# Reordering the last steps of a decode kernel: bias row and its sums ahead of the last PV drain, turned V blocks in pieces of 14 and 10

## The chip, the cores and the metric

The kernel runs on one core of one Trainium2 chip. Kernels are compared only within the same rounds. The metric is the device time of one execution in microseconds (us); several runs are timed and their median is quoted. The profiled execution of the kernel before has a span of 1264.1 us, beside a time of 1265.85 us for that run; times within a trace are counted from the start of its span.

A word on the clock: the profile gives the "granted clock" of TensorE, in parts of its full speed.

## The reference, cut to what matters

One token attends to a cache of 65,536 positions, with 16 query heads on 8 key/value heads of size 256; a small token MLP runs beside it; a gate mixes the two.

```python
q = (x @ wq).reshape(B, Sq, 16, 256).transpose(0, 2, 1, 3)
scores = einsum("bhqd,bhkd->bhqk", q, k) * 256 ** -0.5     # k, v: 8 heads, repeated twice
o = einsum("bhqk,bhkd->bhqd", softmax(scores), v)
a = o.transpose(0, 2, 1, 3).reshape(B, Sq, 4096) @ wo       # -> 448 numbers
b = token_mlp(x)                                            # layernorm, w1, gelu, w2, biases
return g * a + (1 - g) * b                                  # g = sigmoid(sum(x * gate_w))
```

K and V together are about 537 MB in bf16, and each byte is used once.

## The kernel before: the parts that the change touches

The kernel streams K and V through SBUF, 48 chunks of each, and keeps the DMA queue filled. The change concerns only the last V chunk, 80 blocks of 128 keys for the last head pair, and the steps after it. That chunk is loaded in four pieces, and the last two slices of `wo` come behind it:

```python
TURN = 24
TAIL = 4
# ...
edges = [0, nlast - TURN - SB, nlast - TURN, nlast - TAIL, nlast]   # 0, 40, 56, 76, 80
for k in range(len(edges) - 1):
    lo, hi = edges[k] * DH, edges[k + 1] * DH
    sp.dma_start(out=vlast[:, lo:hi], in_=src[:, lo:hi]).then_inc(s_last[k], 16)
# ... then wo for r = 0 and r = 1, 224 KB each, on s_wl[0] and s_wl[1]
```

The first 56 blocks go through TensorE "upright" (P as weights, V streamed, summed in `pv`). VectorE drains `pv` into `og`, and `o_turn` turns that into a column. The last 24 blocks go through "turned": the V block is the weight and P is two columns wide, so that the result lands as a column without any drain. `heads` then scales by the softmax denominators and the gate and writes `oT`, the weights of the 16 last matmuls against `wo`.

```python
upright(edges[0], edges[1])
# ... denominators: den_ps, then rden on VectorE
pe.wait_ge(s_last[1], 16)
upright(edges[1], edges[2]).then_inc(s_fp, 1)
dve.wait_ge(s_fp, 2)
drain_pv(False).then_inc(s_fd, 1)                 # og <- pv + og
dve.tensor_scalar(out=row[:], in0=acc[0:1, 0:D], scalar1=bias[:, 0:1], ...).then_inc(s_fd, 1)
pe.wait_ge(s_fd, 1)
o_turn(2)
pe.wait_ge(s_last[2], 16)
turned(edges[2], edges[3])                        # 20 blocks, 2 matmuls each
pe.wait_ge(s_last[3], 16)
turned(edges[3], edges[4]).then_inc(s_fp, 1)      # 4 blocks
dve.wait_ge(s_fp, 3)
heads().then_inc(s_fd, 1)                         # oT <- o_ps * rden
pe.wait_ge(s_fd, 2)
for a in range(4):                                # the sums of the bias row
    pe.matmul(acc4[32 * a:32 * a + 1, 0:DQ], lhsT=one_f[:, 0:1], rhs=row[:, DQ * a:DQ * (a + 1)],
              start=True, stop=False, tile_position=(0, 32 * a), ...)
pe.wait_ge(s_fd, 3)
for k in range(4):                                # r, cc = divmod(k, 2): 16 matmuls with wo
    # at cc == 0: pe.wait_ge(s_wl[r], 16)
    ...
dve.tensor_copy(out=res[0:97, :], in_=acc4[0:97, 0:DQ])   # the cast; then the store
```

The row (everything but the last head pair: earlier heads, MLP, bias) lies in one partition. The four sums spread it over four partitions of `acc4`, where the `wo` matmuls add to it.

The softmax here doesn't subtract the row's maximum and nothing guards it: scores larger than these inputs give would overflow.

## Time and profile before

| | us |
|---|---|
| time, median of the first 3 runs (range) | 1265.99 (1265.82 to 1266.15) |
| span of the profiled execution | 1264.1 |
| TensorE busy / VectorE busy | 722.2 / 675.3 |
| work after the third V piece has landed, to the cast's end | about 2.8 |

The following lines are from the first two parts of the page. The last two are one figure for each of 40 equal slices: the mean busy share of the 16 DMA engines in tenths, and GB/s.

```profile
span 1264.1 us, 10623 instructions
PE 722.2 (57%) x4296; PEld 276.3 (22%) x4296; DVE 675.3 (53%) x462; ACT 50.1 (4%) x127; POOL 78.5 (6%) x111
DMA  9999999999999999999999999999999999999998
GB/s 407 425 435 429 442 435 424 439 433 432 440 430 426 436 434 437 440 426 434 438 427 438 430 436 436 430 432 436 430 443 429 429 439 434 429 442 430 430 436 348
```

The kernel is a stream of bytes with compute hidden under it. In the stretch that the change touches, only what happens after the last bytes can cost time of its own. This is the end of the chain of waits (start, duration, what). In the lines, PE is TensorE, PEld its weight loads, DVE VectorE, and L751 line 751 of that kernel's file:

```profile
1228.07 30.50 DMA kbuf<-in_A_v_cache_dram
1258.57 0.05 issue
1258.62 1.44 PE misc L751 x48
1260.06 0.48 PE acc L789 x8
1260.54 0.50 PE acc L799 x16
1261.06 0.27 DVE res L806
```

The chain goes from a V piece to the 48 turned matmuls, then the eight TensorE passes of the four bias sums, the `wo` matmuls and the cast. The same stretch in the timeline (start, duration, engine, line, operation, count, idle time before it and what ended that):

```profile
1255.40 0.23 DVE L558 TENSOR_SCALAR rden<-rden,gate 128x2 f32<-128x2 f32 x1
1256.22 0.69 DVE L543 TENSOR_TENSOR og<-pv,og 128x512 f32<-128x512 f32 x1 [0.59 <-PE pv L740]
1256.83 0.66 DVE L776 TENSOR_SCALAR row<-acc,bias 1x448 f32<-1x448 f32 x1
1256.97 1.02 PEld L685 LDWEIGHTS misc<-mask,og 128*128 128x128 f32 x8 [1.30 <-DVE og L543]
1258.61 1.36 PEld L751 LDWEIGHTS misc<-pT,kbuf 128*128 128x128 bf16 x48 [0.62 <-DMA kbuf<-in_A_v_cache_dram]
1259.99 0.55 PE L789 MATMUL acc<-row,one_f 1*1 1x112 f32 x8
1260.09 0.16 DVE L550 TENSOR_TENSOR oT<-misc,rden 128x4 bf16<-128x4 f32 x1 [2.60 <-PE misc L751]
1260.46 0.28 PEld L799 LDWEIGHTS acc<-wo,oT 128*1 128x1 bf16 x16 [0.38 <-DVE oT L550]
1261.06 0.27 DVE L806 CAST res<-acc 97x112 bf16<-97x112 f32 x1 [0.81 <-PE acc L799]
```

Two things can be read here. The 48 turned matmuls start when the 20-block piece lands (when its load's semaphore is full), and run past the landing of the 4-block piece. And `heads` ends at 1260.25, but the `wo` matmuls start only at 1260.46, 0.21 us later; after the drain, which ends at 1256.91, TensorE started within 0.06 us. Between `heads` and `wo`, the sums sit on TensorE.

The view of stretches shows the granted clock at that time (stretch and its length; busy us and instructions of TensorE, of its weight loads, of VectorE, ScalarE and GpSimd; the granted clock; the DMA share; GB/s):

```profile
1258.00:1258.50 0.50, 0.07 (x1) 0.00 (x0) 0.00 (x0) 0.00 (x0) 0.00 (x0) 1.00 0.92 350
1258.50:1259.00 0.50, 0.38 (x14) 0.39 (x15) 0.00 (x0) 0.00 (x0) 0.00 (x0) 0.64 0.59 217
1259.00:1259.50 0.50, 0.50 (x25) 0.50 (x23) 0.00 (x0) 0.00 (x0) 0.00 (x0) 0.50 0.17 50
```

The clock falls to half at about 1258.6.

### The profile page before, as it was taken

The page shows a single profiled execution, that of the slowest core. Times are in us where ns is not written, and L with a number is a line of the kernel's source. Part 1 is how long each engine was busy: PE and PEld are TensorE (multiplying, and loading weights), DVE is VectorE, ACT ScalarE, POOL GpSimd, SP SyncE. Part 2 cuts the span into 40 slices and gives each one's busy share as a digit, 9 for nine tenths or more (in the row PEclk, how much of TensorE's full clock was granted, in tenths as well). Part 3 has the DMA queues.
Part 4 walks back from the last instruction along what each step waited for, and adds up shares of the span by engine and source line. Part 5 has one row for each costly group of instructions (what it writes and reads, how often), then busy time and mean ns, then how long its engine had stood idle before and what let it go on. Part 6 is the DMA issues. An engine that isn't in the chain of part 4 may idle for free. (4 is left out here: it accounts for less than half of the span.)

```text
span 1264.1 us, 10623 instructions
## 1 busy us (share of the span) xinstructions
PE 722.2 (57%) x4296; PEld 276.3 (22%) x4296; DVE 675.3 (53%) x462; ACT 50.1 (4%) x127; POOL 78.5 (6%) x111
## 2 busy tenths in 40 slices
PE   3855656456554665556654564555645656466556
PEld 1311222122221222112221221222212222122212
DVE  5745554465544555455555555464545645465544
ACT  0000000000000000000000000000000000000000
POOL 1001010110110101101011011000000000000000
PEclk9887777878787787777878787777877778778887
DMA  9999999999999999999999999999999999999998
GB/s 407 425 435 429 442 435 424 439 433 432 440 430 426 436 434 437 440 426 434 438 427 438 430 436 436 430 432 436 430 443 429 429 439 434 429 442 430 430 436 348
DMA packets 16840, 544.30 MB, mean 431 GB/s; under 512 B 1856, under 2 KB 3906, under 8 KB 4162
## 3 DMA queue, kind: packets, MB, share of 16 engines
q1 hardware_dynamic: 16744, 544.22, 99.7%
q8 instruction: 2, 0.03, 0.0%
q10 hardware_dynamic: 90, 0.01, 0.0%
q14 instruction: 4, 0.03, 0.0%
HBM read 544.22 MB, written 0.00 MB: 431 GB/s over the span
## 5 line engine op out<-in xcount | busy, mean ns | idle before, releaser
L661 PE MATMUL sc<-kT,qw 128*128 128x512 bf16 x2048 | 573.5, 438 | 482.9 <-PEq L657 482.9
L532 DVE STREAM_TRANSPOSE kT<-kbuf 128x2048 f32<-128x2048 f32 x256 | 572.8, 2285 | 330.1 <-DVEq L524 330.1
L661 PEld LDWEIGHTS sc<-kT,qw 128*128 128x128 bf16 x2048 | 211.1, 108 | 845.1 <-issue 692.8
L675 PE MATMUL pv<-vbuf,pT 128*4 128x512 bf16 x2008 | 121.2, 390 | 28.8 <-PEq L705 28.7
L543 DVE TENSOR_TENSOR og<-pv,og 128x512 f32<-128x512 f32 x40 | 27.7, 692 | 98.5 <-DVEq L524 97.9
L608 ACT ACTIVATE p_t<-sc 128x512 bf16<-128x512 f32 x48 | 28.7, 597 | 1191.9 <-PE sc L661 1191.9
L675 PEld LDWEIGHTS pv<-vbuf,pT 128*4 128x4 bf16 x2008 | 47.1, 88 | 99.3 <-issue 53.8
L589 DVE STREAM_TRANSPOSE pT<-p_t 128x512 bf16<-128x512 bf16 x32 | 22.8, 712 | 74.1 <-DVEq L524 74.1
L635 POOL TENSOR_SCALAR t_b<-t_b 128x448 f32<-128x448 f32 x14 | 7.9, 564 | 359.1 <-ACT t_b L617 359.1
L639 POOL TENSOR_SCALAR t_b<-t_b,hw 128x448 f32<-128x448 f32 x14 | 8.9, 638 | 334.0 <-ACT t_b L625 334.0
L579 DVE STREAM_TRANSPOSE pT<-p_t 128x512 bf16<-128x512 bf16 x8 | 5.7, 712 | 26.9 <-DVEq L524 26.9
L720 PE MATMUL acc<-wo,oT 128*1 128x448 bf16 x28 | 10.1, 504 | 12.7 <-PEq L717 12.7
L644 POOL TENSOR_TENSOR ymix<-ymix,t_b 128x448 f32<-128x448 f32 x14 | 16.1, 1148 | 1.1
L638 POOL TENSOR_TENSOR t_b<-t_b,u_b 128x448 f32<-128x448 f32 x14 | 15.8, 1127 | 1.2
L643 POOL TENSOR_TENSOR t_b<-t_b,u_b 128x448 f32<-128x448 f32 x14 | 15.8, 1126 | 1.2
L542 DVE COPY og<-pv 128x512 f32<-128x512 f32 x8 | 5.5, 692 | 18.9 <-DVEq L524 18.9
L594 DVE STREAM_TRANSPOSE pT<-p_t 128x512 bf16<-128x512 bf16 x8 | 5.7, 712 | 14.9 <-DVEq L524 14.9
L617 ACT ACTIVATE t_b<-h_bc,b1T,w1T 128x448 f32<-128x448 f32 x14 | 10.5, 748 | 0.0
L631 POOL TENSOR_SCALAR u_b<-h_bc,w1T,b1T 128x448 f32<-128x448 f32 x14 | 10.0, 715 | 4.1 <-DVE hw L428 2.7
L608 ACT ACTIVATION_READ_ACCUMULATOR p_t<-sc 128x1 f32 x48 | 9.3, 194 | 0.0
L685 PEld LDWEIGHTS misc<-mask,og 128*128 128x128 f32 x64 | 8.7, 196 | 2.4 <-DVE og L543 1.3
L477 DVE TENSOR_TENSOR qw<-qr,block 128x32 bf16<-128x32 f32 (+1 forms) x18 | 8.6, 561 | 0.1
(86 smaller groups left out, 77.4 us busy)
## 6 DMA issues: line engine op xcount, KB each, us to landing
kbuf<-in_A_k_cache_dram SPq DMA_DIRECT2D x32, 5120.0 KB, 33.2
vbuf<-in_A_v_cache_dram SPq DMA_DIRECT2D x31, 5120.0 KB, 20.4
kbuf<-in_A_k_cache_dram SPq DMA_DIRECT2D x16, 6144.0 KB, 35.7
vbuf<-in_A_v_cache_dram SPq DMA_DIRECT2D x16, 6144.0 KB, 23.5
wo<-in_A_wo_dram SPq DMA_DIRECT2D x7, 448.0 KB, 23.6
vbuf<-in_A_wq_dram SPq DMA_DIRECT2D x1, 3072.0 KB, 10.3
kbuf<-in_A_v_cache_dram SPq DMA_DIRECT2D x1, 2560.0 KB, 26.0
kbuf<-in_A_v_cache_dram SPq DMA_DIRECT2D x1, 1280.0 KB, 30.5
```

The source lines that it names most:

```text
L532: dve.transpose(out=kT[b][:].bitcast(FP32), in_=kn[:, s * SB * 128:(s + 1) * SB * 128]).then_inc(s_kt, 1)
L543: return dve.tensor_tensor(out=og[:], in0=pv[:], in1=og[:], op=ALU.add)
L589: dve.transpose(out=pT[:], in_=p_t[:]).then_inc(s_pt, 1)
L608: ins = act.activation(out=p_t[:], in_=sc[:], func=ACT.Exp, scale=scale, accum_out=den[:, c:c + 1])
L617: ins = act.activation(out=t_b[:], in_=h_bc[:], func=ACT.Square, scale=w1T[:, b:b + 1], bias=b1T[:, b:b + 1],)
L631: lambda: pool.tensor_scalar(out=u_b[:], in0=h_bc[:], scalar1=w1T[:, b:b + 1], scalar2=b1T[:, b:b + 1], op0=ALU.mult, op1=ALU.add,),
L638: lambda: pool.tensor_tensor(out=t_b[:], in0=t_b[:], in1=u_b[:], op=ALU.mult),
L643: lambda: pool.tensor_tensor(out=t_b[:], in0=t_b[:], in1=u_b[:], op=ALU.mult),
L644: lambda: pool.tensor_tensor(out=ymix[:], in0=ymix[:], in1=t_b[:], op=ALU.add),
L661: ins = pe.matmul(sc[:], lhsT=qw[:, q, at:at + 128], rhs=kv[:, :, q // 2, :, q % 2], start=(first and q == 0), stop=(last and q == 7), ski ...
L675: ins = pe.matmul(pv[32 * a:32 * a + 4, :], lhsT=pT[:, k, :, ROW0 + s], rhs=vt[:, j * DH:(j + 2) * DH], start=first and k < 4, stop=last a ...
L720: ins = pe.matmul(acc[0:1, 0:D], lhsT=oT[:, k:k + 1], rhs=wo[:, r, cc, :], start=False, stop=False, skip_group_check=True,)
```

## The change

Its intent is to shorten the chain after the last bytes. The row and its four sums move from between `heads` and `wo` to before the last drain, where both engines wait for V. And the 24 turned blocks come in pieces of 14 and 10, so that more of their matmuls run before the last V piece lands. No byte and no instruction is added or taken away, apart from the waits.

```diff
-TAIL = 4
+TAIL = 10
...
         pe.matmul(
             acc[0:1, 0:D], lhsT=col_f[:], rhs=ymix[:], start=False, stop=True, skip_group_check=True,
-        )
+        ).then_inc(s_fp, 1)
+        dve.wait_ge(s_fp, 1)
+        dve.tensor_scalar(
+            out=row[:], in0=acc[0:1, 0:D], scalar1=bias[:, 0:1], scalar2=None, op0=ALU.add
+        ).then_inc(s_fd, 1)
         take(pe, s_pt)
... (upright, denominators, upright; counts of s_fp one higher)
         drain_pv(False).then_inc(s_fd, 1)
-        dve.tensor_scalar(
-            out=row[:], in0=acc[0:1, 0:D], scalar1=bias[:, 0:1], scalar2=None, op0=ALU.add
-        ).then_inc(s_fd, 1)
         pe.wait_ge(s_fd, 1)
+        for a in range(4):
+            pe.matmul(
+                acc4[32 * a:32 * a + 1, 0:DQ], lhsT=one_f[:, 0:1], rhs=row[:, DQ * a:DQ * (a + 1)],
+                start=True, stop=False, tile_position=(0, 32 * a), skip_group_check=True,
+            )
+        pe.wait_ge(s_fd, 2)
         o_turn(2)
... (turned, turned, heads)
-        pe.wait_ge(s_fd, 2)
-        for a in range(4):
-            pe.matmul(
-                acc4[32 * a:32 * a + 1, 0:DQ], lhsT=one_f[:, 0:1], rhs=row[:, DQ * a:DQ * (a + 1)],
-                start=True, stop=False, tile_position=(0, 32 * a), skip_group_check=True,
-            )
         pe.wait_ge(s_fd, 3)
```

More of the change, by code (lines that the diff above doesn't have):

```diff
@@ L769, in critical @@
         ).then_inc(s_fp, 1)
-        dve.wait_ge(s_fp, 1)
+        dve.wait_ge(s_fp, 2)
         rden_gate(den_ps[:, 0:2])
@@ L773, in critical @@
         upright(edges[1], edges[2]).then_inc(s_fp, 1)
-        dve.wait_ge(s_fp, 2)
+        dve.wait_ge(s_fp, 3)
         drain_pv(False).then_inc(s_fd, 1)
-        dve.tensor_scalar(
-            out=row[:], in0=acc[0:1, 0:D], scalar1=bias[:, 0:1], scalar2=None, op0=ALU.add
-        ).then_inc(s_fd, 1)
         pe.wait_ge(s_fd, 1)
+        for a in range(4):
[4 more added lines that the diff above has]
+        pe.wait_ge(s_fd, 2)
         o_turn(2)
@@ L784, in critical @@
         turned(edges[3], edges[4]).then_inc(s_fp, 1)
-        dve.wait_ge(s_fp, 3)
+        dve.wait_ge(s_fp, 4)
         heads().then_inc(s_fd, 1)
-        pe.wait_ge(s_fd, 2)
-        for a in range(4):
-            pe.matmul(
-                acc4[32 * a:32 * a + 1, 0:DQ], lhsT=one_f[:, 0:1], rhs=row[:, DQ * a:DQ * (a + 1)],
-                start=True, stop=False, tile_position=(0, 32 * a), skip_group_check=True,
-            )
         pe.wait_ge(s_fd, 3)
@@ L804, in critical @@
         ins.then_inc(s_fp, 1)
-        dve.wait_ge(s_fp, 4)
+        dve.wait_ge(s_fp, 5)
         dve.tensor_copy(out=res[0:97, :], in_=acc4[0:97, 0:DQ]).then_inc(s_fd, 1)
```

## The prediction

> **What bounds the kernel.** The page's DMA row reads 9 tenths in all but the last of 40 slices, 431 GB/s on average, while TensorE is busy 57% and VectorE 53% of the span. The chain of waits that ended last is 2.4% DMA (30.50 us for the third piece of the last V chunk) and only about 2.5 us of work behind it. The change moves no byte more or less and acts only after about 1250 of 1264.1 us.
>
> **The tail before** (timeline; issue starts plus the times to landing of the DMA view). The four V pieces are issued at 1227.12, 1227.60, 1228.07 and 1228.55. The 20-block piece lands near 1258.57, the 4-block piece near 1259.23, and the two halves of wo (issued 1229.02 and 1229.49, 30.9 and 31.0 us to landing) near 1260.0 and 1260.4. The 48 turned matmuls start at 1258.61 and are issued in 1.36 us, 28 ns each, then the eight bias-row matmuls at 1259.99, heads on VectorE 1260.09 to 1260.25, the 16 wo matmuls from 1260.46 (issued over 0.28 us), the cast at 1261.06, the store at 1261.36.
>
> **What the change does, costed.**
> 1. Pieces of 14 and 10. Between the last two landings 4 blocks took 0.66 us, so 10 blocks take about 1.6 us (estimate): the 14-block piece lands near 1257.6, the last piece still near 1259.2. The turns of og (1256.97 to 1257.99) now end later than that landing, so 28 turned matmuls run from about 1258.0 and end by 1258.8. The last 20 start at 1259.25 and are issued in 0.57 us: done at 1259.82 instead of 1259.97. Gain for heads: 0.15 us.
> 2. Bias row and its sums ahead. The 0.66 us tensor_scalar runs near 1254.7 to 1255.3 in place of 1256.83; rden then follows by 1255.95, still before the drain's start at 1256.22. The eight sums fall between the last upright matmul (1255.8) and the drain's end (1256.91), where TensorE sat idle 0.80 us. Before, the wo matmuls started 0.21 us after heads ended, while the turns of og started 0.06 us after the drain: the sums held TensorE for about 0.15 us. That is removed.
> 3. The new limit. Points 1 and 2 together would start the wo matmuls near 1260.15, but the second half of wo lands only at 1260.4. Its eight matmuls then start near 1260.45, not 1260.60. So of about 0.3 us freed, I expect only 0.15 us to arrive at the end.
>
> **Clock.** The granted clock fell to 0.50 at about 1258.6 (windows view: 0.64 in 1258.5 to 1259.0, 0.50 after). The Trainium skill, "TensorE: Matmul & The Clock Gate", Part 1, says that the clock is halved after an idle window of about 3.4 us whose phase is free-running; so this may fall elsewhere, worth some tenths either way.
>
> **Predicted:** 1265.8 us, from 1265.0 to 1266.6 (8 in 10), mostly run-to-run spread. Chances: faster by over 2% 0.002, within 2% 0.996, slower by over 2% 0.002.
>
> **What would show it:** the turned matmuls split into 28 and 20 with an idle wait on DMA of about 0.4 us between; no bias-row sums between heads and wo; the wo matmuls split into two groups of eight with a DMA wait on wo between.
>
> **What would make it wrong:** the last pieces landing at other times, the sums delaying the drain or the turns of og, a different clock phase, or the wo landing not being the limit (then 0.3 us).

## The result, and the profile after

| | before | after |
|---|---|---|
| median of 6 runs each, us | 1265.99 | 1265.80 |
| range, us | 1265.80 to 1266.15 | 1265.38 to 1266.00 |
| ratio after / before, 95% interval | | 0.9998 (0.9986 to 1.0011) |

Ratios and intervals here and below are worked out from the fast runs of the same rounds; they are not quite the ratio of the medians quoted. The timed difference is not resolved: the interval is more than ten times as wide as the effect, and in a second set of rounds the order was reversed (below). So the argument has to be made inside the traces.

The end of the chain of waits in the changed kernel:

```profile
1229.03 29.98 DMA kbuf<-in_A_v_cache_dram
1259.01 0.04 issue
1259.05 0.69 PE misc L751 x20
1259.74 0.02 issue
1259.77 0.17 DVE oT L550
1259.94 0.04 issue
1259.98 0.60 PE acc L800 x13
1260.58 0.02 issue
1260.61 0.28 DVE res L807
```

Only 20 turned matmuls are left on the chain, and the sums are gone from it. The timeline of the changed kernel:

```profile
1254.92 0.68 DVE L763 TENSOR_SCALAR row<-acc,bias 1x448 f32<-1x448 f32 x1
1255.88 0.23 DVE L558 TENSOR_SCALAR rden<-rden,gate 128x2 f32<-128x2 f32 x1
1255.99 0.37 PE L782 MATMUL acc<-row,one_f 1*1 1x112 f32 x8
1256.26 0.69 DVE L543 TENSOR_TENSOR og<-pv,og 128x512 f32<-128x512 f32 x1
1257.86 0.89 PEld L751 LDWEIGHTS misc<-pT,kbuf 128*128 128x128 bf16 x28
1259.05 0.59 PEld L751 LDWEIGHTS misc<-pT,kbuf 128*128 128x128 bf16 x20 [0.30 <-DMA kbuf<-in_A_v_cache_dram]
1259.77 0.16 DVE L550 TENSOR_TENSOR oT<-misc,rden 128x4 bf16<-128x4 f32 x1 [2.82 <-PE misc L751]
1259.98 0.31 PEld L800 LDWEIGHTS acc<-wo,oT 128*1 128x1 bf16 x16 [0.35 <-DVE oT L550]
1260.61 0.28 DVE L807 CAST res<-acc 97x112 bf16<-97x112 f32 x1 [0.68 <-PE acc L800]
```

The 48 turned matmuls are split into 28 and 20, with a wait for DMA between. The `wo` matmuls start 0.05 us after `heads` ends (1259.93 to 1259.98). The merged line of the 16 `wo` weight loads hides a hole, which shows when the timeline of that engine is asked for from 1260.15 on:

```profile
1260.19 0.10 PEld L800 LDWEIGHTS acc<-wo,oT 128*1 128x1 bf16 x8
```

The second eight wait for the second half of `wo`. In these traces the semaphore of each of these loads is incremented 16 times, and full with the last; in this trace the last increment for the last half of `wo` comes at 1260.15, and the matmuls that need it start at 1260.19.

**What can be compared between traces.** The last landing itself moves from run to run: 1260.41 in the trace of before, 1260.15 in that of after. That is not the change's doing (see the repeats below). So all traces are compared by what follows the last landing: from it to the start of the cast 0.65 us before and 0.46 us after; from it to the end of the span 3.65 us and 3.45 us. The tail became 0.2 us shorter, 0.016% of the time. The two traces are not at the same clock, though: before fell to half at 1258.64, after at 1259.85. What that is worth is asked below.

### The profile page after: what moved, and what is told of

It reads as the page before. It is cut to its first block, busy times and chain, and to the rows that moved or that the text cites. A ratio compares the mean times of both kernels' runs of the same rounds, so it can differ in the third digit from the quotient of the medians.

```text
span 1263.6 us, 10623 instructions
## 1 busy us (share of the span) xinstructions
PE 718.4 (57%) x4296; PEld 275.5 (22%) x4296; DVE 675.1 (53%) x462; ACT 50.1 (4%) x127; POOL 78.5 (6%) x111
## 5 line engine op out<-in xcount | busy, mean ns | idle before, releaser
L452 PE MATMUL sc<-vbuf,xw 128*128 128x512 bf16 x32 | 9.2, 456 | 0.0
## 6 DMA issues: line engine op xcount, KB each, us to landing
kbuf<-in_A_v_cache_dram SPq DMA_DIRECT2D x1, 1024.0 KB, 27.2
```

The costliest lines, as they stand in the source:

```text
L452: last = e.matmul(q_ps[:], lhsT=xw[:, k, HKV - 1 - n:HKV - 1 - n + 128], rhs=rhs, start=(n == 0 and k == 0), stop=(n == HKV - 1 and k >= K ...
```

## The experiments

Twelve experiments were run. With before and after they make 14 traces of ten different kernels. The table collects their tails. "Last V" is the last increment of the last V piece, "last landing" the last increment of any load; both are read from the trace's semaphore records, as is the time from which the clock is at half. The other columns are worked out from the starts and ends in the timeline, rounded as they are printed, so they can be off by 0.01 us.

| kernel | last landing, us | half clock from | `heads` start after last V | first `wo` matmul after `heads` end | cast after last landing | end of span after last landing |
|---|---|---|---|---|---|---|
| before | 1260.41 | 1258.64 | 0.89 | 0.21 | 0.65 | 3.65 |
| before_again | 1260.36 | 1259.98 | 0.88 | 0.21 | 0.69 | 3.68 |
| after | 1260.15 | 1259.85 | 0.76 | 0.05 | 0.46 | 3.45 |
| after_again | 1260.38 | 1260.52 | 0.76 | 0.05 | 0.41 | 3.40 |
| order_only | 1260.30 | 1257.49 | 0.90 | 0.05 | 0.54 | 3.53 |
| order_only_b | 1260.35 | 1259.07 | 0.91 | 0.05 | 0.51 | 3.50 |
| pieces_only | 1260.54 | 1260.19 | 0.76 | 0.12 | 0.47 | 3.47 |
| pieces_only_b | 1260.53 | 1260.54 | 0.75 | 0.05 | 0.45 | 3.45 |
| sums_twice | 1260.51 | 1260.45 | 0.87 | 0.31 | 0.77 | 3.78 |
| tail16 | 1260.46 | 1260.13 | 1.08 | 0.05 | 0.75 | 3.74 |
| tail20 | 1260.24 | 1257.94 | 1.32 | 0.05 | 0.93 | 3.93 |
| wo_first | 1260.30 | 1258.74 | 0.77 | 0.06 | 1.59 | 4.59 |
| wo_three | 1260.47 | 1259.56 | 0.78 | 0.05 | 0.43 | 3.42 |
| before_warm | 1260.58 | 1262.03 | 0.87 | 0.06 | 0.36 | 3.36 |

The two theories at the outset: (T) the sums held TensorE, the last turned matmuls held `heads`, and once both are shorter the last half of `wo` is the limit; (R) one of the two parts, or mere semaphore latency, accounts for it all. All runs computed the right result.

### The parts alone, a repeat, and the sums doubled

**order_only**: the changed kernel with the old sizes.

```diff
-TAIL = 10
+TAIL = 4
```

> The new order with pieces of 20 and 4. Theory (the sums held TensorE between heads and the wo matmuls, and the last wo landing is the new limit): the gap from the end of heads to the first wo matmul falls from 0.21 us (before) to 0.06 us; the last turned matmul still ends about 0.75 us or more after the 20-block piece plus, so heads starts about 1.5 us after the 20-block piece lands, as before (1258.57 to 1260.09); the wo matmuls start about 1.7 us after it, close to or after the landing of the last wo half, so the cast starts 0.50 to 0.55 us after that landing (before 0.65, after 0.46). Rival (the 0.21 us was semaphore latency or the wo landing, and the smaller last piece did all the work): the gap stays 0.21 us and the cast starts 0.65 us after the landing. Time: 0.1 us under before by the theory, equal by the rival; both inside the noise of 0.2 us.

Measured: 1265.89 us against 1265.82 for before (ratio 1.0000, interval 0.9987 to 1.0014). The gap after `heads` is 0.05 us, `heads` is as late as before, the cast comes 0.54 us after the last landing. This is what (T) expects:

```profile
1260.02 0.16 DVE L550 TENSOR_TENSOR oT<-misc,rden 128x4 bf16<-128x4 f32 x1 [3.18 <-PE misc L751]
1260.24 0.28 PEld L800 LDWEIGHTS acc<-wo,oT 128*1 128x1 bf16 x16 [0.34 <-DVE oT L550]
```

**pieces_only**: the kernel before with the new sizes.

```diff
-TAIL = 4
+TAIL = 10
```

> The old order with pieces of 14 and 10. Theory: the turned matmuls split into 28 and 20, heads starts 0.75 us after the last V piece lands (before 0.86), but the bias-row sums still hold TensorE for about 0.37 us from there, so the wo matmuls start 0.21 us after heads ends; with heads 0.1 us earlier against the landings the first group of wo matmuls starts near the last wo landing, and the cast starts 0.50 to 0.55 us after it. Rival (pieces alone do it all): gap 0.06 us and cast at 0.46 us, as in the changed kernel.

Measured: 1265.89 us against 1265.82 (ratio 1.0001). `heads` moved as expected, but the gap was 0.12 us and not 0.21, and the cast came 0.47 us after the last landing. The pieces alone reached the same place as the whole change. The expectation missed by the gap: the sums cost less here. This trace was at full clock until 1260.19, that of before at half clock from 1258.64. That was the first hint of a cause which the prediction had not put at this place.

**after_again**: the changed kernel, unchanged.

> The changed kernel once more. Theory: its own tail is reproduced against the landings: two groups of eight wo matmuls, the second 0.04 us after the last wo landing, the cast 0.46 us after that landing, while the absolute landing time moves by some tenths of a us from run to run. Rival (the 0.26 us earlier last landing in the changed kernel's trace is its own doing, from the larger last piece): the last wo landing stays about 30.1 us after its issue again, against 30.9 us before. Time 1265.8 us, 0.1 to 0.3 us under before.

Measured: 1266.00 us against 1265.82 (ratio 1.0001), so here the changed kernel is the later one by 0.2 us. Together with the first rounds this says only that the times do not resolve the change. The tail is reproduced: cast 0.41 us after the last landing. The landings of `wo` are 31.4 us after issue, against 30.1 in the first look at the same kernel; the rival, that larger pieces make the bytes land earlier, falls.

**sums_twice**: the kernel before with the sums done twice in their old place (the second overwrites the first).

```diff
-for a in range(4):
+for a in (0, 1, 2, 3, 0, 1, 2, 3):
     pe.matmul(acc4[32 * a:32 * a + 1, 0:DQ], lhsT=one_f[:, 0:1], ...)
```

> The kernel before with the four bias-row sums done twice in their old place (the second overwrites the first, the result is the same). Theory (the sums hold TensorE): heads is not moved, the wo matmuls start about 0.35 us later against it, 0.55 to 0.6 us after heads ends instead of 0.21, and the cast starts 1.0 us after the last wo landing instead of 0.65; time up by about 0.3 us. Rival (the sums hide under heads and the gap is latency): nothing moves by more than 0.05 us.

Measured: 1266.07 us against 1265.82 (ratio 1.0001). The gap after `heads` grew to 0.31 us and the cast came 0.77 us after the last landing: the sums do hold TensorE. But it is 0.1 us more than in before, not the 0.35 us expected. Again the clocks differ: this trace is at full clock until 1260.45. From the first sum to the first `wo` matmul, 16 passes took 0.58 us here (1260.11 to 1260.69), where eight took 0.47 us in before at half clock.

### A repeat of before, and the limit behind the change

**before_again**: the kernel before, unchanged.

> The kernel before once more, to see its tail at another phase of the clock (half clock from 1258.64 in its first trace, full clock to 1260 in three of the later traces). If the tail is at full clock: turned matmuls still 28 to 29 ns each (the trace of the changed kernel at full clock shows the same 29 ns), the gap from heads to the wo matmuls 0.12 us as in pieces_only instead of 0.20, and the cast 0.55 to 0.60 us after the last landing. If at half clock: 0.20 and 0.65 again. The last landing may lie 0.3 us to either side. Time as before, within 0.2 us.

Measured: 1265.99 us against 1265.82 for the same kernel (ratio 1.0003), which shows how large a difference of nothing is. The clock fell at 1259.98, just as the sums began at 1259.97, so they ran at half clock again: gap 0.21, cast 0.69 us after the landing. The `wo` landings came 30.2 us after their issue, as early as in the first look at the changed kernel. So the case "sums at full clock in the old order" was still missing.

**wo_first**: the changed kernel with both `wo` slices asked for before the last two V pieces.

```diff
-for k in range(len(edges) - 1):       # the four V pieces
+for k in (0, 1):                      # two V pieces
     ...
 # wo, r = 0 and r = 1
+for k in (2, 3):                      # the other two V pieces
+    lo, hi = edges[k] * DH, edges[k + 1] * DH
+    sp.dma_start(out=vlast[:, lo:hi], in_=src[:, lo:hi]).then_inc(s_last[k], 16)
```

> The changed kernel with both wo halves asked for ahead of the last two V pieces, so that wo is never waited for and the 10-block piece lands last. Theory (the end of all bytes is fixed and the tail is what work remains after the last landing): last landing unchanged near 1260.3, then 20 turned matmuls, heads 0.76 us after it, all 16 wo matmuls, the cast 1.55 us after the last landing instead of 0.46; time up by about 1.1 us, to 1266.9. Rival (the wait for wo costs the tail 0.1 to 0.2 us and removing it gains that): time down by 0.1 to 0.2 us.

Measured: 1266.88 us (1266.69 to 1267.17) against 1265.82, 1.06 us more between the medians, with every run above every run of before. Its ratio is 1.0010; the 95% interval quoted with it (0.9996 to 1.0023) still holds 1. The last landing stayed at 1260.30, and its timeline shows the whole chain behind it:

```profile
1260.34 0.61 PEld L754 LDWEIGHTS misc<-pT,kbuf 128*128 128x128 bf16 x20 [0.70 <-DMA kbuf<-in_A_v_cache_dram]
1261.29 0.28 PEld L803 LDWEIGHTS acc<-wo,oT 128*1 128x1 bf16 x16 [0.34 <-DVE oT L553]
1261.88 0.28 DVE L810 CAST res<-acc 97x112 bf16<-97x112 f32 x1 [0.65 <-PE acc L803]
```

The end of the bytes is fixed, and the time is that end plus whatever still has to follow it. Of the two orders, the one with `wo` last is the better.

**tail16 and tail20**: the changed kernel with turned pieces of 8 and 16, and of 4 and 20.

```diff
-TAIL = 10
+TAIL = 16        # and 20 in the other
```

> The changed kernel with turned pieces of 8 and 16. Theory (heads waits for the turned matmuls of the last V piece, 29 ns each): heads starts 1.1 us after the last V landing (0.76 with pieces of 14 and 10), the wo matmuls follow at 1.3 us in one run of 16 with no wait for wo, the cast starts 0.75 to 0.8 us after the last wo landing instead of 0.41 to 0.46; time up by 0.3 us. Rival (the sizes do not matter once the sums are out of the way): cast at 0.46 us.

> The changed kernel with turned pieces of 4 and 20. Theory: heads 1.35 us after the last V landing, the cast about 1.0 us after the last wo landing; time up by 0.5 to 0.6 us over the changed kernel. Rival: as for pieces of 8 and 16, nothing moves.

Measured: 1265.98 and 1266.00 us against 1265.82 (both ratios 1.0003). In the traces `heads` starts 1.08 and 1.32 us after the last V landing and the cast comes 0.75 and 0.93 us after the last landing: 0.3 and 0.5 us more than in the changed kernel, as expected. The times moved by less than expected and stay within the noise. In the trace of the 20-block piece, 40 matmuls wait for it:

```profile
1259.08 1.15 PEld L751 LDWEIGHTS misc<-pT,kbuf 128*128 128x128 bf16 x40 [1.07 <-DMA kbuf<-in_A_v_cache_dram]
1260.36 0.16 DVE L550 TENSOR_TENSOR oT<-misc,rden 128x4 bf16<-128x4 f32 x1 [3.62 <-PE misc L751]
1260.57 0.28 PEld L800 LDWEIGHTS acc<-wo,oT 128*1 128x1 bf16 x16 [0.34 <-DVE oT L550]
```

### The parts again, less work behind the last landing, and the clock

**order_only_b and pieces_only_b**: the same two kernels, one look each.

> The new order with pieces of 20 and 4 again, one look. If the first look holds: 0.05 us from heads to the wo matmuls, heads 0.9 us after the last V landing, the cast 0.54 us after the last wo landing at half clock, some hundredths less at full clock.

> The old order with pieces of 14 and 10 again, one look. If the first look holds: 0.12 us from heads to the wo matmuls at full clock, 0.2 at half clock; heads 0.76 us after the last V landing; the cast 0.47 us after the last wo landing at full clock and 0.5 to 0.55 at half clock.

Measured: 1265.63 and 1265.76 us, one run each. The order alone gave a gap of 0.05 us and the cast 0.51 us after the last landing, much as in its first look. The pieces alone with the sums in their old place gave a gap of 0.05 us, not the 0.12 that the first look had shown; the clock was full until 1260.54, through the whole stretch:

```profile
1260.04 0.37 PE L789 MATMUL acc<-row,one_f 1*1 1x112 f32 x8
1260.36 0.57 PE L799 MATMUL acc<-wo,oT 128*1 128x112 bf16 x16
```

The sums take 0.37 us here and 0.55 us in the trace of before. `wo` starts 0.32 us after the first sum. `heads` needs about as long itself: it started at 1260.14, 0.10 us after that sum, took 0.16 us, and TensorE followed within 0.05 us. At full clock the sums just fit under `heads`.

**wo_three**: the changed kernel with the last half of `wo` in two loads, one for each `cc`, so that 4 instead of 8 matmuls wait for the last landing.

```diff
-sp.dma_start(out=wo[:, 1, :, :] ..., in_=... "(p c) n -> p (c n)").then_inc(s_wl[1], 16)
+for cc in range(2):
+    sp.dma_start(out=wo[:, 1, cc, :], in_=... "(p c) n -> p c n" [:, cc, :]).then_inc(s_wl[1 + cc], 16)
...
-            if cc == 0:
-                pe.wait_ge(s_wl[r], 16)
+            if k != 1:
+                pe.wait_ge(s_wl[r + (k == 3)], 16)
```

> The changed kernel with the last half of wo loaded in two parts, so that only 4 of the 16 wo matmuls wait for the last landing instead of 8. Theory (what follows the last landing sets the tail): the cast comes 0.35 to 0.40 us after the last landing instead of 0.41 to 0.46, but 128 lines of 1792 bytes become 256 of 896 bytes and one more transfer is issued, so the last landing may come 0.1 to 0.3 us later and take the gain back. Time within 0.2 us of the changed kernel.

Measured: 1265.70 us against 1265.82 (ratio 0.9999). The cast came 0.43 us after the last landing, no better than 0.41 and 0.46, so the hoped-for 0.05 us did not show. (This trace is at half clock from 1259.56, so the 0.46 of after is the like one; 0.03 us between two single traces decides nothing.) The last landing, 1260.47, was not outside the range of the others.

**before_warm**: the kernel before, old order and old pieces, with seven matmuls that nobody reads in TensorE's idle time.

```diff
+def warm(n):
+    for _ in range(n):
+        pe.matmul(sc[:], lhsT=one_b[:], rhs=kT[0][:, 0:512], start=True, stop=True, ...)
 upright(edges[0], edges[1])
+warm(2)
 ...
 upright(edges[1], edges[2]).then_inc(s_fp, 1)
+warm(3)
 ...
 o_turn(2)
+warm(2)
 pe.wait_ge(s_last[2], 16)
```

> The kernel before with seven matmuls of 128x512 that nobody reads, put into TensorE's idle time in the tail (2, 3 and 2 of them), to keep the granted clock at 1.0 through the bias-row sums. The old order and the old pieces of 20 and 4 stay. Theory A (the sums in their old place hold up the wo matmuls at half clock alone: 0.48 us from first sum to first wo matmul in both traces of before, 0.32 us in the second look at the old order with pieces of 14 and 10): if the clock stays at 1.0 until 1260.3, the first wo matmul comes 0.05 us after heads ends and 0.32 to 0.33 us after the first sum, and the cast 0.50 to 0.55 us after the last landing instead of 0.65 to 0.69. Theory B (the sums hold TensorE at either clock, so the order by itself is worth 0.15 us): 0.2 us after heads and 0.48 us after the first sum at full clock too. Turned matmuls at 27 to 29 ns under both. If the clock falls all the same, the look decides nothing.

Measured: 1265.72 us against 1265.90 (ratio 0.9999, interval 0.9985 to 1.0013). The clock stayed full until 1262.03, past the whole tail. The sums sit between `heads` and `wo` as in before, and yet:

```profile
1260.16 0.37 PE L799 MATMUL acc<-row,one_f 1*1 1x112 f32 x8
1260.27 0.16 DVE L550 TENSOR_TENSOR oT<-misc,rden 128x4 bf16<-128x4 f32 x1 [2.58 <-PE misc L751]
1260.49 0.23 PEld L809 LDWEIGHTS acc<-wo,oT 128*1 128x1 bf16 x16 [0.23 <-DVE oT L550]
1260.94 0.28 DVE L816 CAST res<-acc 97x112 bf16<-97x112 f32 x1 [0.51 <-PE acc L809]
```

`wo` starts 0.33 us after the first sum and 0.06 us after `heads`. That is theory A of this run, and theory B falls. The cast missed its expectation (0.50 to 0.55): it comes 0.36 us after the last landing, the shortest of all 14 traces and 0.3 us less than in before. In this trace old code on a full clock has a shorter tail than the changed code, which ran with the clock at half from 1259.85 or 1260.52. Part of that is the `wo` matmuls themselves: from the first of them to the cast it took 0.45 us here, 0.60 us in before. The rest shows when the weight loads are asked for from 1260.6 on:

```profile
1260.62 0.10 PEld L809 LDWEIGHTS acc<-wo,oT 128*1 128x1 bf16 x8
```

The second eight start 0.04 us after the last landing (1260.58), just as in the changed kernel. So at full clock the kernel before already waits for the last half of `wo`, and in this trace the change would have had nothing left to take away ahead of that wait. Whether the changed kernel with the same seven matmuls would be shorter still was not run. Nothing of this can be told from the timed medians.

## Why the prediction was right

The prediction was right: 1265.8 us foretold and 1265.80 measured, within its range. As the noise is as large as the effect, the time alone proves little, and that the median was hit to 0.01 us is luck: in the second set of rounds the changed kernel was at 1266.00 against 1265.82. The steps can be checked in the traces.

1. **The stream is the bound, and the change acts only behind it.** Right. The page of the changed kernel has the same DMA share in all 40 slices, and moving `wo` ahead (wo_first) showed in the median that what follows the last landing is paid in full.
2. **Pieces of 14 and 10.** Right. Foretold were a 14-block landing near 1257.6 and a gain for `heads` of 0.15 us. The landing was at 1257.43, and `heads` starts 0.76 us after the last V landing instead of 0.89 and 0.88.
3. **Bias row and sums.** Right in the trace that the prediction was read from, but the reason was incomplete. The 0.15 us that "the sums held TensorE" exists only at half clock, where `wo` follows the first sum after 0.47 us. At full clock it follows after 0.32 to 0.33 us, which `heads` takes anyway, so the sums are hidden (pieces_only_b and before_warm). The prediction knew of the clock and said it was "worth some tenths either way", which is its right size (0.3 us, before_again against before_warm), but did not say where it would act.
4. **The new limit.** Right. The second eight `wo` matmuls start 0.04 us after the last half of `wo` lands. The two parts do not add up: against 0.65 and 0.69 us for before, the order alone left 0.51 to 0.54 us behind the last landing, the pieces alone 0.45 to 0.47, both together 0.41 to 0.46. The clocks differ among these: no trace has the pieces alone with all of the sums at half clock, so what they are worth there without the order is not shown.
5. **The size of what arrives.** Foretold were 0.15 us; the cast comes 0.65 and 0.69 us after the last landing in the two traces of before, and 0.46 us in the first of after, so about 0.2 us with the `wo` matmuls at half clock in all three. (The 0.41 us of after_again has the clock at full until 1260.52, after these matmuls have started, so it is not a like one.) The mis-sized term is the second group of `wo` matmuls. The prediction moved its start from 1260.60 to 1260.45 and took the rest as equal. The start was right: 0.19 us after the last landing in before, 0.04 us in after, 0.15 us less. But from there to the cast it took 0.46 us in before and 0.41 us in after. In before the four batches of four matmuls start at 1260.46, 1260.51, 1260.60 and 1260.70, while after the pause in the changed kernel the two last ones start at 1260.19 and 1260.24. All of these ran at half clock. Three other traces at half clock without a pause (tail16, tail20, wo_first) have the same distances from batch to batch as before: 0.05, 0.09 and 0.09 us. That the batches after a pause start closer together because less is in flight is a reading of these starts; no run was made for it.
6. **Where the drain starts.** Foretold near 1256.2, measured at 1256.26. But here the change gives something back: the second V piece had landed at 1255.31, 0.95 us earlier, against 0.70 us in before. The row's 0.68 us now stand ahead of the denominators on VectorE, and `rden` ended only at 1256.11, where it ended at 1255.63 before. With 14 blocks in the third piece there was still room for that: 0.30 us of waiting ahead of the last 20 matmuls, and 0.11 us in the repeat.

## What to carry to other kernels

When a stream of loads fills the time, ask only what is still to be done after the last landing, and measure two versions against that landing in their traces: a change of 0.2 us that eleven timed runs could not show is plain there. Several waits that end close together give less together than the sum of each; look for the next one before adding up gains. And look at the granted clock before blaming an instruction for its duration: four small sums were free at full clock and cost 0.15 us at half.

## What the Trainium skill lacked or had wrong

- "TensorE: Matmul & The Clock Gate", Part 1, says that the clock goes to half after a window of about 3.4 us without activity, the window being free-running. The traces agree on the window: the last four whole stretches between changes in the first trace are 10.24, 13.65, 10.24 and 17.07 us long, 3, 4, 3 and 5 times 3.41. What the section lacks is how much activity, and of what kind, keeps the clock full. In sums_twice TensorE was busy for 2.78 of the 3.41 us before the clock fell at 1260.45 (the ends of matmuls are modelled in the trace, so this is rough), 2.51 us of it with the turned matmuls of two columns and the small turns of `og`:

```profile
1257.04:1260.45 3.41, 2.78 (x72) 2.63 (x72) 1.12 (x3) 0.00 (x0) 0.00 (x0) 1.00 0.56 211
```

  Seven matmuls of 512 columns in the tail (before_warm) kept it full until 1262.03. The rule behind that was not measured.
- The same page, section "Back-to-back issue gap", gives a floor of about 25 ns from one small matmul to the next at full clock. The turned matmuls, each with its own 128x128 weight load, came every 26.5 ns at full clock (before_warm, 48 of them) and every 27.2 ns at half (before). So the spacing is near that floor, though no run separates the floor from the weight load that goes with each of these matmuls. The runs add that the half clock hardly changes this spacing; the section has no floor for the half clock.
- No page gives the time that one-row fp32 matmuls on four column tiles hold TensorE. Four of them (eight passes) held it for 0.47 us at half clock, from the first to the next matmul of another kind, and for no more than 0.32 us at full clock.
- "DMA: Bandwidth & Descriptors", "Latency and other measured facts", says that two of the 16 engines are usually slower, and gives no size; its best guess at the cause is for loads whose descriptors software writes, while the loads here are on a queue that the profile calls hardware_dynamic. In each of the 14 traces the last of the 16 increments of the last load came 1.0 to 1.5 us after the middle one, and up to 1.0 us after the second last (pieces_only_b). The traces read here do not name the engine, so whether it is one of those two is not shown. That lag is larger than everything that the change could gain, and nothing here was tried against it.
